# Attention and two MoE layers on one core: the last routing in another order with VectorE's subtractions, and the small tokens' block with its copy and its transposes moved

## The chip, the cores and the metric

The kernel runs on 1 core of a Trainium2 chip. The metric is the device time in microseconds (us) of one execution. Engines are called as in the profile: PE is TensorE, DVE is VectorE, ACT is ScalarE, POOL is GpSimd, SP is SyncE, which issues most DMAs. PSUM is the memory that PE writes; its banks are tiles such as `psT`, `psH`, `psO`, `psf`, `psR` here, and SBUF is the memory that the engines and the DMAs share.

## The reference

Attention over 4 x 8 heads of 576 positions with 64 columns each (half of the heads with a local mask, half with a strided one) gives 2304 tokens of 512 columns. Two mixture-of-experts layers follow, each with 8 experts of which a token takes one:

```python
def _moe_ref(x, w_skip, w_gate, w1, w2):            # layer 1
    do_compute = x @ w_skip > 0
    xc = x[do_compute]
    logits = xc @ w_gate
    e_idx = np.argmax(logits, axis=1)
    gate_w = softmax(logits)[arange, e_idx]
    for e in range(8):
        m = e_idx == e
        y[m] = gate_w[m, None] * (np.maximum(xc[m] @ w1[e], 0.0) @ w2[e])
    out = x.copy(); out[do_compute] = xc + y
def _moe2_ref(x, modality_id, w_gate, modality_bias, w1, w2):   # layer 2
    logits = x @ w_gate + modality_bias[modality_id]
    ...  # the same choice of one expert for every token, no residual
    out[m] = gate_w[m, None] * (np.maximum(x[m] @ w1[e], 0.0) @ w2[e])
```

w1 is 512 x 1024 and w2 is 1024 x 512 for each expert.

## The kernel before, in words

**Products.** A float32 number is split into two numbers of the type fp32r, a high and a low part: `x = xh + xl`, `w = wh + wl`. Each product is three matmuls: `wh` by `xh`, `wl` by `xh`, `wh` by `xl`. An expert's two weight matrices come as 8 pieces of 128 x 1024 numbers (512 KB). SP loads a piece into one of six buffers `raw`; `hi(c)` (L301) makes `wh` from it with a copy on ACT; `lo(c)` (L305) makes `wl` with the subtraction `raw - wh`, on DVE or on POOL, and then calls `ahead(1)`, which issues the load of a further piece into a buffer that has come free. `pieces(i)` gives the pairs of `hi` and `lo` of the weights number `i`.

**Stages.** Attention writes the tokens to DRAM (`xbuf`). A token that layer 1 skips goes on to layer 2 at once, so the routing also forms lists for layer 2. `drain` runs when attention's last tile is through; it covers about the stretch from 128 to 167 us. In it three things are interleaved by the turns of a loop. First, `route(1)`, the last routing: it is a generator, and each `next` runs it up to the next `yield`. It finds the greatest logit of each token as a one-hot matrix `r_oh` (L555 to L558), then counts on PE which place the token takes in its expert's list (`rk`, L565 to L571; `r_sel`, L574), then the gates (`r_gs`, `ent`), the number of tokens of each expert (`cnt`, L593) and the plan of the blocks (`plan1`), then the places `r_val`, `r_vi`, `r_pc`, then one-hot matrices of them (`ra`, L626, `r_b`, `rb`, L658) and by matmuls with these the lists of token numbers (`ls`, L643 and L664; `list`, L666). Between them, `later(n)` issues up to `n` small DVE instructions of the planning that were put off (all at L160). Second, `fill`, which works through two full tiles of the favourite expert of layer 2 (`psf`, `hfh`, `hfl`; matmuls L1455 and L1467). Third, 7 of the 8 pieces of the second weight slot, which layer 1 needs; `wstep()` runs one `hi` or one `lo`.

The loop of `drain` gives in each turn one step of the routing, two `wstep`s and as many groups of `fill` as `RUNS` says. Each engine runs its instructions in the order in which they are issued here. After `drain` the first block of layer 1 gathers the tokens `xgA` by the list, transposes them (`psT`, L1268), splits them (`xh` on ACT, `xl` on DVE, L1264) and multiplies (`psH`, `psO`, L1279).

**Few tokens.** A block of layer 1 has a tile of 128 tokens and, where an expert's list goes just beyond it, up to 32 "few" tokens. These go through the weights in float32, unsplit, beside the tile of the block (`few1`). `FEW1` says ahead of which matmul of the tile (0 to 47) each step of theirs stands. `timed` sorts all steps of a block by that number; steps with one number keep their order, and steps put off from the block before (`self.defer`) stand first among equals. Among these are the ranks of the few tokens of the block before (`carry`, L1621, which reads the bank `psT` of the few tokens, called T3 in the program) and its list (`list`, L1630, which reads the bank `psR`). Steps of the few tokens that matter here: `first` (L1125) copies their columns from `psR` to `x`; `l1` (L1130) multiplies by the first weights into the bank T3; `relu` (L1135) reads this bank on ACT, and then PE transposes `x` into the same bank (L1136); `trh` transposes the result of the relu (L1268). The loop body of a block runs for the kinds of blocks in `USUAL`; on these inputs three blocks have few tokens.

Of the kernel before, what the change touches and what calls it, by code (L numbers as in the profile page):

```python
# [65 lines left out]
HI1 = (0, 0, 7, 15, 21, 26, 35, 39)  # L66
LO1 = (1, 1, 10, 15, 25, 28, 37, 42)
TL1 = (6, 11, 22, 22, 24, 28, 32, 34, 45)
FEW1 = (0, 4, 4, 7, 9, 19, 21, 22, 24, 27, 31, 34, 34, 37, 47)
MISC1 = (8, 22, 27, 41, 43)  # L70
RAW6 = 11
SOON = (0, 0, 1, 1, 1, 2, 1, 1, 0)
# [1 line left out]

USUAL = ("one", "one", "two", "one", "few", "few", "few", "one")
KINDS = [{"one": (62, 0), "two": (63, 2), "few": (62, MARK)}[n] for n in USUAL]
RUNS = (1, 3, 2, 3, 1, 2, 6, 4, 4, 3)
SLOTS = ("A0", "B0", "A1", "B1", "C0", "C1")
FIRST, REST = (("A1", "B1"), ("A0", "B0")), ("C0", "C1")
OUT = float(2 ** 23)  # L80
# [1 line left out]
SBT = NTILE // 2  # L82
# [84 lines left out]
class Net:  # L167
# [255 lines left out]
    def drain(self, fill):  # L423


        tc = self.tc
        self.inx.close()
        pool = self.ctx.enter_context(tc.tile_pool(name="slot1", bufs=1, side="right", reuse_waits="tile"))
        self.wsl[1] = [self.whalf(1, i, pool) for i in range(2)]
        self.raw += [pool.tile([P, FF], F32, name=f"raw{i}", tag=f"raw{i}") for i in range(3, 6)]  # L430
        self.ahead(3)
        self.rp = self.flx.enter_context(tc.tile_pool(name="rt", bufs=1, reuse_waits="tile"))
        self.wside = [op for p in self.pieces(1, pool=range(8))[:7] for op in p]
        runs = list(RUNS)
        while self.side or self.rside:
            self.step(1 - self.ofree)
            self.wstep()
            self.wstep()
            self.run(fill, runs.pop(0) if runs else 3)
        self.run(fill, 99)  # L440
        while self.wside:
            self.wstep()
        self.flx.close()
        self.apx.close()

# [81 lines left out]
    def route(self, sb, lt):  # L527

        nc, ps, ap = self.nc, self.ps, self.ap
# [6 lines left out]
        def t(nm, w, dt=F32):  # L536
            return self.sm("r_" + nm, w, dt, pool=ap)
# [34 lines left out]
                         self.offb.unsqueeze(1).to_broadcast([P, SBT, W]), start=False, stop=True)  # L572
        sel = t("sel", [SBT, W])
        nc.vector.tensor_tensor(sel.rearrange("p j n -> p (j n)"), rk, ohf, op=ALU.mult)  # L574

        gs, ent = t("gs", [SBT, 2]), self.ent[:, j0:j0 + SBT]
        nc.vector.tensor_reduce(gs.rearrange("p j g -> p (j g)"), fl(ex), axis=AX.X, op=ALU.add)
# [10 lines left out]
        else:  # L588
            with nc.allow_low_precision("small integers"):
                nc.vector.tensor_reduce(self.carry, oh.rearrange("p j n -> p n j"), axis=AX.X, op=ALU.add)  # L590
        yield 1
        o4 = self.obank(f"cnt{sb}")
        nc.tensor.matmul(o4[:, :2 * E], self.onb, self.carry, start=True, stop=True)  # L593
        if sb:
            cnt = self.sm("cnt", 2 * E, pool=self.rp)
            nc.vector.tensor_copy(cnt, o4[:, :2 * E])
            self.plan1(cnt)
            yield 1
        else:
            m = self.sm("c_n", E + 1)  # L600
            nc.vector.scalar_tensor_tensor(m[:, :E], o4[:, E:2 * E], 0.0, self.foh, ALU.add, ALU.mult, accum_out=m[:, E:])
            nc.vector.tensor_scalar(self.full, self.cst("thr")[:, 1:1 + FULL], m[:, E:], None, ALU.is_le)
            nc.vector.tensor_reduce(self.nfull, self.full, axis=AX.X, op=ALU.add)
        val, vi, pc = t("val", SBT), t("vi", [3, SBT], I32), t("pc", [2, SBT])
        later = self.bg.issue
        nc.vector.tensor_reduce(val, sel, axis=AX.X, op=ALU.add)
        later(2)
        nc.vector.tensor_copy(vi[:, 0], val)
        later(2)
        nc.vector.tensor_scalar(vi[:, 1], vi[:, 0], P - 1, None, ALU.bitwise_and)  # L610
        later(2)
        nc.vector.tensor_scalar(vi[:, 2], vi[:, 0], 7, None, ALU.logical_shift_right)
        later(2)
        nc.vector.tensor_copy(pc, vi[:, 1:])
        later(2)
        yield 1
# [13 lines left out]
        if sb:  # L630

            b0, b1 = t("b0", [SBT, NTILE]), t("b1", [SBT, NTILE], F32R)
            nc.vector.tensor_tensor(b0, bc(col, NTILE), iota[:, :NTILE].unsqueeze(1).to_broadcast([P, SBT, NTILE]),
                                    op=ALU.is_equal)
            later(2)
            nc.vector.tensor_tensor(b1, b0, bc(tid, NTILE), op=ALU.mult)
            later(2)
            for g in range(ng):
                mk_a(g)
            yield 1  # L640
            o3 = self.obank("ls0")
            for j in range(SBT):
                nc.tensor.matmul(o3[:, :NTILE], aa[j // n][:, j % n], b1[:, j], start=j == 0, stop=j == SBT - 1)  # L643
            f = t("f", [2, NTILE])
            nc.vector.tensor_tensor(f[:, 0], self.list1[:, :NTILE], o3[:, :NTILE], op=ALU.add)
            later(2)
            nc.vector.tensor_scalar(f[:, 1], f[:, 0], 0.0, self.cst("dummy"), ALU.is_equal, ALU.mult)
            later(2)
            nc.vector.scalar_tensor_tensor(self.li[0], f[:, 0], -1.0, f[:, 1], ALU.add, ALU.add)
            later(2)  # L650
            self.gather("A0", self.li[0][:, 0:1])
        for g in range(ng):
            bb = []
            if not sb:
                mk_a(g)
            for j in range(g * n, g * n + n):
                b = ap.tile([P, NC2], F32R, name=f"rb{sb}{j}", tag="rb", bufs=n)
                nc.vector.tensor_scalar(b, iota, col[:, j:j + 1], tid[:, j:j + 1], ALU.is_equal, ALU.mult)  # L658
                later(2)
                bb.append(b)  # L660
            yield 1
            o3 = self.obank(f"ls{sb}{g}")
            for i, b in enumerate(bb):
                nc.tensor.matmul(o3[:, :NC2], aa[g][:, i], b, start=i == 0, stop=i == n - 1)  # L664
            if sb or g:
# [446 lines left out]
    def few1(self, k, free):  # L1112

        nc, b, Q, i = self.nc, self.bk["T3"], 2 * P, k % 2
        xg, ix = self.xs[f"C{i}"]["g"], self.fwi[:, 2 * i:2 * i + 1]

        t = self.xs[f"B{1 - i}"]["g"]
        hs, y, x = t[:, :Q], t[:, Q:Q + P], t[:, Q + P:Q + 2 * P]
# [245 lines left out]
    def tile_few(self, k, slot, idx, conv, start, end):  # L1364
# [519 lines left out]
```

## Time and profile before

| | |
|---|---|
| time, median of 3 runs | 566.18 us (562.84 to 567.45) |
| the profiled execution | 565.65 us |
| its span, first to last instruction | 563.8 us |
| mean granted clock of PE, as a share of full speed | 0.966 |
| busy: PE, DVE, ACT, POOL | 503.2, 326.2, 244.2, 112.0 us |

The difference of 1.85 us between the profiled execution and its span lies outside the instructions. The chain that ended last is made up of 55% PE, 16% DVE, 12% DMA, 8% issue and 7% ACT. PE is busy for most of the span, but the shares are averages over stages. In `drain` and at the ends of blocks other engines set the pace, and there PE waits.

### The profile page before, as it was taken

How to read it: one execution, taken by the hardware profiler on the slowest of the kernel's cores; microseconds unless marked ns; L12 is line 12 of the kernel's file. 1: busy time of each engine (PE TensorE's matmuls, PEld its weight loads, DVE VectorE, ACT ScalarE, POOL GpSimd, SP SyncE). 2: the span in 40 equal slices, each digit the busy share in tenths (PEclk: the TensorE clock that was granted, in tenths of full speed). 3: DMA queues.
4: the chain of work that ended last, by engine and by line, in shares of the span. 5: the costliest groups of instructions: out<-in, count | busy, mean ns of one | idle time of the engine just before them, and what ended most of it. 6: DMA issues, size and time to landing. Idle time of an engine off the chain costs nothing.

```text
span 563.8 us, 11022 instructions
## 1 busy us (share of the span) xinstructions
PE 503.2 (89%) x3959; PEld 398.7 (71%) x3959; DVE 326.2 (58%) x909; ACT 244.2 (43%) x539; POOL 112.0 (20%) x129
## 2 busy tenths in 40 slices
PE   5998998986687989999898987989999999999992
PEld 2677666775575669666565666979987788899981
DVE  1567689747879689696967795656522122223121
ACT  0888696653227556366456562135211121111120
POOL 4200000106515222122202032041211202020210
PEclk9999899998889899999999998989999999999997
DMA  8996885326517788387656575038231741120110
GB/s 205 341 337 205 255 284 181 90 73 237 155 38 257 270 289 270 130 292 227 208 187 223 169 234 199 20 121 287 85 80 44 258 179 39 40 76 20 58 41 20
DMA packets 32807, 94.76 MB, mean 168 GB/s; under 512 B 6192, under 2 KB 11282, under 8 KB 32720
## 3 DMA queue, kind: packets, MB, share of 16 engines
q1 hardware_dynamic: 26464, 75.23, 40.6%
q0 software_dynamic: 5824, 18.01, 9.7%
q8 instruction: 39, 0.64, 0.5%
q10 hardware_dynamic: 432, 0.49, 0.4%
q14 instruction: 48, 0.39, 0.2%
HBM read 81.72 MB, written 12.62 MB: 167 GB/s over the span
## 4 chain that ended last, share of the span: by engine, by line
PE 55%; DVE 16%; DMA 12%; issue 8%; ACT 7%; POOL 1%; DVEq 0%; ACTq 0%; POOLq 0%
PE psH L1455 11%; PE psT L1467 7%; PE psO L1467 7%; DMA xgB<-xbuf,li 6%; PE psH L1279 4%; PE psT L1455 4%; DVE wl L305 3%; PE psT L1268 3%; PE o L1778 2%; PE pt L1760 2%; DMA xbuf<-x1p,pidx 2%; ACT p L1749 2%; PE psf L1455 2%; DMA neg<-in_neg 1%; ACT wh L301 1%
## 5 line engine op out<-in xcount | busy, mean ns | idle before, releaser
L305 DVE TENSOR_TENSOR wl<-raw,wh 128x1024 fp32r<-128x1024 f32 (+1 forms) x89 | 98.9, 1123 | 17.4 <-ACT wh L301 17.2
L301 ACT CAST wh<-raw 128x1024 fp32r<-128x1024 f32 (+1 forms) x96 | 96.0, 1021 | 7.1 <-issue 4.3
L1461 ACT ACTIVATE hh<-psH 128x256 fp32r<-128x256 f32 x45 | 17.3, 384 | 94.0 <-PE psH L1455 94.0
L1462 DVE SCALAR_TENSOR_TENSOR hl<-psH,hh 128x256 fp32r<-128x256 f32 x45 | 18.9, 424 | 63.3 <-ACT hh L1461 63.3
L1749 ACT ACTIVATE p<-s,mx 128x96 f32<-128x96 f32 (+2 forms) x152 | 41.2, 373 | 0.9 <-DVE r L1785 0.9
L1455 PE MATMUL psH<-xl,wh 128*128 128x256 f32 x192 | 32.4, 289 | 2.0 <-DVE xl L1264 2.0
L1455 PE MATMUL psH<-xh,wl 128*128 128x256 f32 x192 | 33.5, 291 | 0.2 <-issue 0.2
L1455 PEld LDWEIGHTS psH<-xh,wh 128*128 128x128 f32 x192 | 29.2, 191 | 4.4 <-ACT xh L1263 1.0
L1763 ACT COPY pts<-pt 96x512 f32<-96x512 f32 (+4 forms) x48 | 22.9, 495 | 21.0 <-PE pt L1760 20.5
L1455 PE MATMUL psH<-xh,wh 128*128 128x256 f32 x192 | 31.1, 284 | 0.8 <-ACT xh L1263 0.8
L1455 PEld LDWEIGHTS psH<-xl,wh 128*128 128x128 f32 x192 | 27.1, 194 | 3.0 <-DVE xl L1264 2.4
L1455 PEld LDWEIGHTS psH<-xh,wl 128*128 128x128 f32 x192 | 27.6, 196 | 1.5 <-issue 1.5
L1424 POOL DMA_INDIRECT out_dram<-x1p,li x8 | 8.0, 1004 | 96.1 <-DVE x1p L1423 94.2
L1467 PE MATMUL psO<-wh,hh 128*128 128x512 f32 x60 | 25.1, 419 | 0.0
L1279 PE MATMUL psO<-wh,hl 128*128 128x512 f32 x72 | 24.2, 429 | 0.8 <-DVE hl L1264 0.8
L1602 POOL DMA_INDIRECT xbuf<-x1p,pidx x8 | 8.9, 1114 | 79.3 <-DVE xgB L1609 42.9
L1279 PE MATMUL psO<-wl,hh 128*128 128x512 f32 x72 | 24.6, 425 | 0.0
L1264 DVE TENSOR_TENSOR xl<-psT,xh 128x512 fp32r<-128x512 f32 x29 | 19.9, 688 | 8.1 <-ACT xh L1263 8.1
L1279 PE MATMUL psH<-wl,xh 128*128 128x512 f32 x72 | 24.5, 421 | 0.0
L1760 PE MATMUL pt<-cst,p 128*96 128x128 f32 (+2 forms) x152 | 23.5, 276 | 0.9 <-ACT xT L1813 0.9
L1467 PE MATMUL psT<-wh,hh 128*128 128x512 f32 x60 | 23.9, 398 | 0.0
L1467 PE MATMUL psT<-wh,hl 128*128 128x512 f32 x60 | 23.7, 395 | 0.0
(451 smaller groups left out, 1164.5 us busy)
## 6 DMA issues: line engine op xcount, KB each, us to landing
raw<-in_w SPq DMA_DIRECT2D x104, 512.0 KB
qk<-in_lqk SPq DMA_DIRECT2D x8, 592.0 KB
qk<-in_sqk SPq DMA_DIRECT2D x8, 576.0 KB
v<-in_lv SPq DMA_DIRECT2D x8, 438.8 KB
v<-in_sv SPq DMA_DIRECT2D x8, 325.0 KB
xbuf<-xl SPq DMA_DIRECT2D x4, 576.0 KB
xbuf<-xs SPq DMA_DIRECT2D x12, 108.0 KB
xbuf<-xs SPq DMA_DIRECT2D x8, 126.0 KB
```

Of the source, the lines that this page charges most:

```text
L301: nc.scalar.copy(placed(wh[:, c % 4, q], c), turned(self.rawtile(8 * i + c)[:, q], c))
L305: (nc.gpsimd if c in pool else nc.vector).tensor_tensor(placed(wl[:, c % 4, q], c), turned(self.rawtile(8 * i + c)[:, q], c), placed(wh[:, ...
L1264: nc.vector.tensor_tensor(l, src, h.bitcast(F32), op=ALU.subtract)
L1268: self.nc.tensor.transpose(bank[:, k * P:(k + 1) * P], src[:, k * P:(k + 1) * P], self.ident)
L1279: return [lambda i=i, a=a, b=b: self.nc.tensor.matmul(out, a, b, start=first and i == 0, stop=last and i == n - 1) for i, (a, b) in enumer ...
L1455: return [lambda i=i, k=k, w=w, x=x: nc.tensor.matmul(hb[f % nb], w[:, k, c], x[:, k], start=i == 0 and k == 0, stop=i == 2 and k == 3) fo ...
L1461: nc.scalar.activation(h, hb[f % nb], AF.Relu)
L1462: nc.vector.scalar_tensor_tensor(l, hb[f % nb], 0.0, h.bitcast(F32), ALU.max, ALU.subtract)
L1467: return [lambda i=i, j=j: nc.tensor.matmul(ob[t], hp[i][:, c], m[j], start=f == 0 and i + j == 0, stop=f == FF // P - 1 and i == 1) for i ...
L1749: nc.scalar.activation(self.p[:rows, h, c], self.s[:rows, h, c], AF.Exp, scale=0.125, bias=self.mx[:rows, h, n:n + 1])
L1760: nc.tensor.transpose(pt[:w, (n - n0) * rows:(n - n0 + 1) * rows], self.p[:rows, h, n * w:(n + 1) * w], net.ident[:rows, :rows])
L1763: nc.scalar.copy(pts[:w, :m * rows], pt[:w, :m * rows])
```

## The change

The change has two parts. In `drain` the seven subtractions of the second weight slot run on DVE and no longer on POOL, and three tables say how many groups of `fill`, copies and subtractions each turn has. The last routing (`sb` = 1) works out the tokens' places right after `r_sel`; the gates come after them, and the count matmul and the plan come after the one-hot matrices. `later(4)` takes the place of `later(2)` behind each `rb` and each `list`.

In the few tokens' block, `first` has the number -1, so that it stands ahead of the steps that were put off with number 0; `trh` has 11 where it had 9; and in `relu` PE's transposing of `x` is issued ahead of ACT's relu.

```diff
-FEW1 = (0, 4, 4, 7, 9, 19, 21, 22, 24, 27, 31, 34, 34, 37, 47)
+FEW1 = (-1, 4, 4, 7, 11, 19, 21, 22, 24, 27, 31, 34, 34, 37, 47)
...
-RUNS = (1, 3, 2, 3, 1, 2, 6, 4, 4, 3)
+
+RUNS = (1, 3, 2, 3, 4, 5, 5, 5)
+HIS = (0, 1, 1, 1, 1, 1, 1, 1)
+LOS = (0, 0, 1, 0, 1, 1, 2, 2)
...
-        self.wside = [op for p in self.pieces(1, pool=range(8))[:7] for op in p]
-        runs = list(RUNS)
+        his, los = [list(ops) for ops in zip(*self.pieces(1)[:7])]
+        runs = [*zip(RUNS, HIS, LOS)]
         while self.side or self.rside:
+            n, nh, nl = runs.pop(0) if runs else (3, 7, 7)
             self.step(1 - self.ofree)
-            self.wstep()
-            self.wstep()
-            self.run(fill, runs.pop(0) if runs else 3)
+            for ops, m in ((his, nh), (los, nl)):
+                for op in ops[:m]:
+                    op()
+                del ops[:m]
+            self.run(fill, n)
...
         nc.vector.tensor_tensor(sel.rearrange("p j n -> p (j n)"), rk, ohf, op=ALU.mult)
+        val, vi, pc = t("val", SBT), t("vi", [3, SBT], I32), t("pc", [2, SBT])
+        later = self.bg.issue
+
+        def places():
+            nc.vector.tensor_reduce(val, sel, axis=AX.X, op=ALU.add)
+            nc.vector.tensor_copy(vi[:, 0], val)
+            nc.vector.tensor_scalar(vi[:, 1], vi[:, 0], P - 1, None, ALU.bitwise_and)
+            nc.vector.tensor_scalar(vi[:, 2], vi[:, 0], 7, None, ALU.logical_shift_right)
+            nc.vector.tensor_copy(pc, vi[:, 1:])
+        if sb:
+
+            places()
...
             for g in range(ng):
                 mk_a(g)
+            yield 1
+            o4 = self.obank(f"cnt{sb}")
+            nc.tensor.matmul(o4[:, :2 * E], self.onb, self.carry, start=True, stop=True)
+            cnt = self.sm("cnt", 2 * E, pool=self.rp)
+            nc.vector.tensor_copy(cnt, o4[:, :2 * E])
+            self.plan1(cnt)
             yield 1
...
                 nc.vector.tensor_scalar(b, iota, col[:, j:j + 1], tid[:, j:j + 1], ALU.is_equal, ALU.mult)
-                later(2)
+                later(4)
...
         def relu():
+            nc.tensor.transpose(b[:, P + Q:], x, self.ident)
             nc.scalar.activation(self.halves(hs), self.turn(h), AF.Relu)
-            nc.tensor.transpose(b[:, P + Q:], x, self.ident)
             nc.scalar.copy(y, b[:, P + Q:])
```

Line numbers after the change are 3 to 8 higher. On DVE in `drain`, around the one-hot `r_oh` of the last routing, before:

```order
L557 TENSOR_TENSOR r_eq<-r_eq,r_mx 128x144
L558 TENSOR_TENSOR r_oh<-r_eq,r_act 128x144
L1462 SCALAR_TENSOR_TENSOR hfl<-psf_1828,hfh 128x256
L574 TENSOR_TENSOR r_sel<-rk_2010,r_oh 128x144
L577 TENSOR_REDUCE r_gs<-r_ex 128x18
L578 TENSOR_SCALAR r_gs<-r_gs 128x18
```

The same place on DVE now:

```order
L563 TENSOR_TENSOR r_eq<-r_eq,r_mx 128x144
L564 TENSOR_TENSOR r_oh<-r_eq,r_act 128x144
L308 TENSOR_TENSOR wl_1938<-raw_70,wh_1937 128x1024
L1470 SCALAR_TENSOR_TENSOR hfl<-psf_1828,hfh 128x256
L580 TENSOR_TENSOR r_sel<-rk_2005,r_oh 128x144
L585 TENSOR_REDUCE r_val<-r_sel 128x9
L586 CAST r_vi<-r_val 128x9
```

The first subtraction (`wl`) has come in behind `r_oh`, ahead of the split `hfl` and of `r_sel`, and the places `r_val`, `r_vi` follow `r_sel` where the gates `r_gs` followed.

On DVE at the end of `drain`, from the last `rb` to the last `list` (the names at L160 are the put-off planning), before:

```order
L658 TENSOR_SCALAR rb_2269<-csta,r_pc 128x288
L160 TENSOR_REDUCE f_v<-f_junk 128x1
L160 TENSOR_TENSOR f_junk<-c_foh,cnt 128x8
L666 TENSOR_TENSOR list_118<-list_118,ls_2284 128x288
L160 TENSOR_REDUCE f_m<-f_junk 128x1
```

The same place on DVE now:

```order
L666 TENSOR_SCALAR rb_2255<-csta,r_pc 128x288
L163 TENSOR_REDUCE f_v<-f_junk 128x1
L163 TENSOR_TENSOR f_junk<-c_foh,cnt 128x8
L163 TENSOR_REDUCE f_m<-f_junk 128x1
L163 SCALAR_TENSOR_TENSOR f_m<-c_nfull,f_m 128x1
L308 TENSOR_TENSOR wl_1940<-raw_1943,wh_1939 128x1024
L308 TENSOR_TENSOR wl_1940<-raw_70,wh_1939 128x1024
L674 TENSOR_TENSOR list_118<-list_118,ls_2286 128x288
```

The last two of the seven subtractions stand between the last `rb` and the last `list`; behind that come the rest of the planning and then `xl` of the first block, as before.

On PE in a block with few tokens, from the last few-token matmul of the first weights to the transposes of `trh` (the `psT_2313` written from `xgB` is the bank T3), before:

```order
L1130 MATMUL psT_2313<-raw_68,xgB_2331 32x256 x4
L1279 MATMUL psH_2316<-wl_65,xh_2337 128x512 x2
L1268 MATMUL psT_2310<-cst,x1p 128x128 x4
L1279 MATMUL psH_2316<-wl_65,xh_2337 128x512
L1136 MATMUL psT_2313<-cst,xgB_2331 128x128
L1279 MATMUL psH_2316<-wl_65,xh_2337 128x512
L1279 MATMUL psH_2316<-wh_64,xl_2342 128x512
L1268 MATMUL psT_2313<-cst,xgB_2331 128x128 x2
```

The same place on PE now:

```order
L1138 MATMUL psT_2313<-raw_68,xgB_2331 32x256 x4
L1287 MATMUL psH_2316<-wl_65,xh_2337 128x512 x2
L1276 MATMUL psT_2310<-cst,x1p 128x128 x4
L1287 MATMUL psH_2316<-wl_65,xh_2337 128x512
L1143 MATMUL psT_2313<-cst,xgB_2331 128x128
L1287 MATMUL psH_2316<-wl_65,xh_2337 128x512
L1287 MATMUL psH_2316<-wh_64,xl_2342 128x512 x3
L1276 MATMUL psT_2313<-cst,xgB_2331 128x128 x2
```

The transposing of `x` stands at the same place among PE's instructions, but it no longer waits for the relu, which now waits for it; the two transposes of `trh` stand behind four of the tile's matmuls where they stood behind two. On POOL, the seven rows of L305 ahead of the gather of `xgA` (L1254) are gone. On ACT the copy L1125 stands where it stood.

## Rows read from the trace of the kernel before

**Rows 1.** Part 1 of the page: busy time, share of the span, instructions.

```profile
PE 503.2 (89%) x3959; PEld 398.7 (71%) x3959; DVE 326.2 (58%) x909; ACT 244.2 (43%) x539; POOL 112.0 (20%) x129
```

**Rows 2.** Timeline of PE, 128 to 190 us: start, us, instructions, [idle before <-releaser].

```profile
137.51 0.30 PE L565 MATMUL rk<-r_oh,ltb 128*128 128x144 bf16 x1 [5.40 <-DVE r_oh L558]
...
153.85 2.26 PE L643 MATMUL ls<-r_b,ra 128*128 128x18 f32 x9 [4.54 <-DVE ra L626]
...
183.10 0.66 PE L1268 MATMUL psT<-cst,xgA 128*128 128x128 f32 x4 [3.03 <-DMA xgA<-xbuf,li]
```

**Rows 3.** Timeline of POOL, 125 to 185 us.

```profile
127.52 9.77 POOL L305 TENSOR_TENSOR wl<-raw,wh 128x1024 fp32r<-128x1024 f32 x4 [16.71 <-ACT wh L301]
144.16 7.09 POOL L305 TENSOR_TENSOR wl<-raw,wh 128x1024 fp32r<-128x1024 f32 x3 [6.87 <-ACT wh L301]
...
175.40 1.72 POOL L1254 DMA_INDIRECT xgA<-xbuf,li  x1 [4.03 <-DVE li L821]
```

**Rows 4.** DVE by source line: xcount, ns min/median/max, first and last start, forms.

```profile
L555 DVE SCALAR_TENSOR_TENSOR r_eq<-r_L,cst x2: 309/1373/2437, 83.4 to 130.2; 128x144 f32<-128x144 f32 x2
...
L557 DVE TENSOR_TENSOR r_eq<-r_eq,r_mx x2: 309/1178/2048, 84.1 to 133.0; 128x144 f32<-128x144 f32 x2
...
L558 DVE TENSOR_TENSOR r_oh<-r_eq,r_act x2: 307/1345/2383, 84.4 to 135.1; 128x144 bf16<-128x144 f32 x2
...
L612 DVE TENSOR_SCALAR r_vi<-r_vi x2: 165/1278/2391, 90.4 to 148.9; 128x9 int32<-128x9 int32 x2
...
L160 DVE TENSOR_TENSOR more<-more,one x2: 153/1262/2370, 144.2 to 151.2; 128x8 f32<-128x8 f32 x2
...
L160 DVE TENSOR_SCALAR one<-f x1: 2324/2324/2324, 146.6 to 146.6; 128x8 f32<-128x8 f32 x1
```

**Rows 5.** Windows: start:end, us, busy PE, PEld, DVE, ACT, POOL, PEclk, DMA share, GB/s.

```profile
129.11:169.23 40.12, 28.48 (x143) 24.10 (x142) 32.83 (x107) 10.39 (x16) 17.88 (x10) 0.83 0.42 139
...
180.70:184.10 3.40, 1.00 (x7) 0.92 (x8) 2.43 (x5) 1.73 (x3) 0.60 (x3) 1.00 0.96 363
184.10:187.50 3.40, 3.40 (x11) 2.31 (x9) 2.52 (x3) 0.87 (x2) 0.00 (x0) 0.50 1.02 402
```

**Rows 6.** Groups by line and form: xcount, busy us, mean ns of one, idle before.

```profile
L305 DVE TENSOR_TENSOR wl<-raw,wh 128x1024 fp32r<-128x1024 f32 x73 | 87.9, 1219 | 14.6 <-ACT wh L301 14.5
...
L305 POOL TENSOR_TENSOR wl<-raw,wh 128x1024 fp32r<-128x1024 f32 x7 | 16.9, 2445 | 23.6 <-ACT wh L301 23.6
```

**Rows 7.** Waits of DVE, 129.11 to 169.23 us: us in total, times, longest us.

```profile
DVE hfl L1462 <- ACT hfh L1461: 4.9, 3, 2.4
DVE list L666 <- PE ls L664: 1.3, 3, 0.7
DVE r_sel L574 <- PE rk L571: 0.8, 1, 0.8
```

**Rows 8.** Waits by source line, L1135 and L1125: who waited for them (us, times).

```profile
  PE psT L1136: 2.4, 3
...
  PE psT L1130: 4.5, 3
```

**Rows 9.** Timeline of PE, 272 to 284 us, a block with few tokens.

```profile
277.23 1.93 PE L1130 MATMUL psT<-raw,xgB 128*32 128x256 f32 x32 [1.71 <-ACT xgB L1125]
...
281.28 0.33 PE L1136 MATMUL psT<-cst,xgB 128*128 128x128 f32 x1 [0.79 <-ACT xgB L1135]
...
282.22 0.72 PE L1279 MATMUL psH<-wh,xl 128*128 128x512 f32 x2
```

**Rows 10.** Timeline of DVE and ACT, 270 to 285 us, the same block.

```profile
275.83 0.29 DVE L1630 TENSOR_TENSOR list<-list,psR 128x144 f32<-128x144 f32 x1
...
276.98 0.14 DVE L1621 TENSOR_TENSOR carry<-carry,psT 128x8 f32<-128x8 f32 x1
...
276.16 0.27 ACT L1125 COPY xgB<-psR 128x128 f32<-128x128 f32 x1 [2.46 <-DVE list L1630]
280.84 0.39 ACT L1135 ACTIVATE xgB<-psT 128x256 f32<-128x256 f32 x1
```

More of the change, by code (lines that the diff above doesn't have):

```diff
@@ L432, in drain @@
         self.rp = self.flx.enter_context(tc.tile_pool(name="rt", bufs=1, reuse_waits="tile"))
-        self.wside = [op for p in self.pieces(1, pool=range(8))[:7] for op in p]
-        runs = list(RUNS)
+        his, los = [list(ops) for ops in zip(*self.pieces(1)[:7])]
+        runs = [*zip(RUNS, HIS, LOS)]
         while self.side or self.rside:
+            n, nh, nl = runs.pop(0) if runs else (3, 7, 7)
             self.step(1 - self.ofree)
-            self.wstep()
-            self.wstep()
-            self.run(fill, runs.pop(0) if runs else 3)
+            for ops, m in ((his, nh), (los, nl)):
[3 more added lines that the diff above has]
+            self.run(fill, n)
         self.run(fill, 99)
-        while self.wside:
-            self.wstep()
+        for op in his + los:
+            op()
         self.flx.close()
@@ L590, in route @@
                 nc.vector.tensor_reduce(self.carry, oh.rearrange("p j n -> p n j"), axis=AX.X, op=ALU.add)
[L591 to L597, printed above, removed]
+        if not sb:
             yield 1
-        else:
+            o4 = self.obank(f"cnt{sb}")
+            nc.tensor.matmul(o4[:, :2 * E], self.onb, self.carry, start=True, stop=True)
             m = self.sm("c_n", E + 1)
@@ L603, in route @@
             nc.vector.tensor_reduce(self.nfull, self.full, axis=AX.X, op=ALU.add)
-        val, vi, pc = t("val", SBT), t("vi", [3, SBT], I32), t("pc", [2, SBT])
-        later = self.bg.issue
-        nc.vector.tensor_reduce(val, sel, axis=AX.X, op=ALU.add)
-        later(2)
[L608 to L616, printed above, removed]
+            places()
+            yield 1
         n, ng = 3, SBT // 3
@@ L640, in route @@
             yield 1
+            o4 = self.obank(f"cnt{sb}")
+            nc.tensor.matmul(o4[:, :2 * E], self.onb, self.carry, start=True, stop=True)
+            cnt = self.sm("cnt", 2 * E, pool=self.rp)
+            nc.vector.tensor_copy(cnt, o4[:, :2 * E])
+            self.plan1(cnt)
+            yield 1
             o3 = self.obank("ls0")
@@ L658, in route @@
                 nc.vector.tensor_scalar(b, iota, col[:, j:j + 1], tid[:, j:j + 1], ALU.is_equal, ALU.mult)
-                later(2)
+                later(4)
                 bb.append(b)
@@ L666, in route @@
                 nc.vector.tensor_tensor(self.list1[:, :NC2], self.list1[:, :NC2], o3[:, :NC2], op=ALU.add)
-                later(2)
+                later(4)
             else:
                 nc.vector.tensor_copy(self.list1[:, :NC2], o3[:, :NC2])
-                later(2)
+                later(4)
         if not sb:
```

## The prediction, made before the change was run

> **What bounds the kernel now.** I read the busy shares first: PE is busy 503.2 of the span [rows 1], so time can only be won where PE stands still or where it is slowed. The timeline of PE shows such places in `drain`: it stands 5.40 us ahead of `rk`, for DVE's `r_oh`, and 4.54 us ahead of the first `ls`, for DVE's `ra` [rows 2]. So in `drain` the bound is DVE's chain of routing instructions. In the window from the first of them to the start of the first block's `xl`, 40.12 us, DVE is busy 32.83 us and PE 28.48 at a mean clock of 0.83 [rows 5].
>
> The next view tells why DVE is so busy. The same source lines run twice in the kernel, for each routing once. `r_eq`, `r_oh` and their like take 0.31 us in the one and 2.05 to 2.44 in the other; small instructions of 0.15 to 0.17 us take 2.32 to 2.39 there [rows 4]. These six long ones start between 130.2 and 149 us, all inside the two runs of POOL's subtractions, 127.52 to 137.3 and 144.16 to 151.25 [rows 3], and none is longer than one such subtraction, 2.445 us [rows 6]. I take it that POOL's subtraction holds DVE's instruction back until it is through.
>
> Behind `drain` the lead must not be lost again. PE's next long wait is 3.03 us for the second gather of `xgA` [rows 2], which POOL issues after 4.03 us of waiting for DVE's `li` [rows 3]. So what comes early there is what DVE's chain makes early; a PE that arrives earlier than that only waits longer.
>
> **Subtractions from POOL to DVE.** Released are the excesses of the six instructions, maximum less minimum of each row, and for the sixth, which ran once, less 0.165 of its like: 2.13 + 1.74 + 2.08 + 2.23 + 2.22 + 2.16 = 12.55 us [rows 4]. Added are seven subtractions of 1.219 us [rows 6], 8.53 us. DVE's work in the window is then 32.83 - 12.55 + 8.53 = 28.81 us. Of its idle 7.29 us, 7.0 are waits in three groups: 4.9 for ACT's `hfh`, 1.3 for PE's `ls`, 0.8 for `rk` [rows 7]; 0.29 are small gaps and stay. If no wait stays, the window takes 29.1 us and 11.0 are saved; if all stay, 36.1 and 4.0 are saved. In the new order a subtraction stands between `r_oh` and `r_sel`, which covers the 0.8, and subtractions stand ahead of three of the `hfl`, 3.66 us against the 4.9, which leaves 1.24. I let the 1.3 at `ls` stay whole. Then 2.5 stay, the window takes 31.6 us, and **8.5 us** are saved. PE's work in the window, 28.5 us with two stretches at half clock in it, is shorter than this and loses its two long waits; it stays beside DVE's.
>
> The other moves of this part cost little by themselves. The places go ahead of the gates, five short instructions ahead of seven, so `ra` and the first `ls` come earlier on DVE's chain; the sum above has all of this inside, as it counts work and not order. The count and the plan come later; what waits for them are the put-off instructions, which have no waiter before the end of `drain`. SP's loads of further weight pieces follow each subtraction, and the last two subtractions stand behind the last `rb`, some 2 us before `xl`. They put 2.4 us ahead of the last `list` and `xl`, and their two loads come late beside the start of the first block. The 2.4 is in the sum of DVE's work; the loads are in a rival below. POOL loses 16.9 us of work [rows 6] and nobody waits for it in `drain`, so its gathers come no later.
>
> **Relu and transposes.** PE's transpose (L1136) waits for ACT's relu three times, 2.4 us together [rows 8], once 0.79 [rows 9]. After the change it waits for nothing but PE's own work, which was through at 281.28 - 0.79 = 280.49. The relu then waits for it. It started at 280.84 [rows 10] because ACT came to it then, later than such a transpose needs, so the relu still ends at about 281.23. What is late next is `trh`, which reads the relu's result. It stands behind four matmuls now; two take 0.72 us [rows 9], so four take 1 us at least with the transpose, and end past 281.4: no wait. I count the whole 2.4 less 0.05 for handing over, **2.35 us**. The bounds are 0, if the wait only moves to `trh`, and 2.4.
>
> **The copy ahead of put-off work.** The waits by source line give 4.5 us in three waits of PE for the copy L1125 [rows 8], 1.71 of it in the block shown [rows 9]. That suggests a gain, but the rows say otherwise. The copy started at 276.16, right behind DVE's `list` of 275.83 to 276.12, on which it waited 2.46 us, and it ended at 276.43; PE's matmul began only at 277.23, behind `carry` (276.98 to 277.12), which reads the bank that the matmul writes [rows 10]. Neither `list` nor `carry` is moved, and on ACT the copy stands where it stood. I count **0**; the other end is -4.5, nearer to nothing in these rows.
>
> The waits view and a rule differ here, in sentences that the sum can do without. The Trainium skill, PSUM — Partial Sum Buffer, section "PSUM bank collisions raise a hardware error", says that accesses of two engines to one bank must be kept apart by a semaphore per bank, reads against reads too. By the waits view alone the edit would be worth up to 4.5 us; by that rule the copy has to wait for the reader of `psR` and the matmul for the reader of T3, wherever the copy is written. The trace agrees with the rule by the 0.11 us between `carry`'s end and the matmul's start.
>
> **The sum**, against the profiled execution of 565.65 us (0.5 below the median of 566.18, which I take as the same): 565.65 - 8.5 - 2.35 + 0 = **554.8 us**.
>
> **Rivals.** (B) The start of layer 1 gives part back. From 180.70 to 184.10 PE was busy 1.00 us of 3.40, and the 3.40 us behind it ran at half clock with PE busy throughout [rows 5]. That is 1.7 us lost. At the end of `drain` PE now has two subtractions of DVE to sit through and may be as sparse, and the last loads of weights come later. One or two such stretches cost 1.7 to 3.4 us: 556.5 to 558.2. Against it speaks that `drain` had two stretches at half clock, of which one may go. The Trainium skill, TensorE: Matmul & The Clock Gate, section "HAM oscillation — how this bites in real kernels", describes the same as a rule: a PE that waits for data is put back to 1.2 GHz (of 2.4) and starts its next work slow; the trace agrees by the clock of 0.50 behind the sparse stretch.
>
> (C) DVE's waits all stay, because subtractions wait for ACT's `wh` (they did for 14.6 us in 73 cases, 0.2 each [rows 6]) and the `hfl` for PE as before. Then 4.0 are saved: 565.65 - 4.0 - 2.35 = 559.3.
>
> (D) More goes than I count: no wait stays on DVE, 565.65 - 11.0 - 2.35 = 552.3, and with the 4.5 of the copy 547.8. For it: the waits of `hfl` come from a PE that was itself held up or at half clock.
>
> (E) The other side: POOL is not what stretches DVE's instructions; they wait for something else that stays. Then DVE's unbroken chain gets 8.53 us more, 565.65 + 8.53 - 2.35 = 571.8, or 566.9 if the 4.9 of `hfl` take some of it up. It decides from the point where less than 8.5 of the 12.55 us are released. Against it: six of six long instructions lie beside POOL's work.
>
> (F) The edit doesn't do what it says: the copy comes no earlier. This is in the forecast.
>
> **How the numbers follow.** My forecast has 55%, with a range of its own of 552.5 to 556.5; B 18%, C 9%, D 8%, E 3%, and 7% for what I don't see. The range holds the forecast, B and C, 82%: 550 to 560 us, its low end between D's two values. A measurement of this kernel tells about 1%, 5.7 us, from no change. Below 560.5 lie the forecast, B, D and nearly all of C: 88% faster. Within 1% are the rest of C, half of E and part of the unseen, 8%; slower 4%.
>
> **What would show it.** In the profile after: `r_eq`, `r_oh`, `r_vi` at 0.31 and 0.17 us in both routings; seven more DVE subtractions of about 1.2; the window from DVE's first routing instruction to `xl` 31 to 32 us long; no wait of 4 us or more of PE in `drain`; the second gather of `xgA` 8 to 9 us earlier; no wait of PE for L1135's relu; PE's wait at the few-token matmul unchanged at 4 to 5 us in three. It would be wrong if small DVE instructions are still stretched, if `wl` on DVE waits for `wh` by several us, or if the blocks of layer 1 are longer by half-clock stretches than before.

## The result

The changed kernel takes 549.98 us (median of 4 runs, 548.6 to 551.21) beside 565.72 us before: ratio 0.9726, 95% interval 0.9676 to 0.9776. Timed again (e9), it gave 0.9729 (0.9677 to 0.978). That is some 15 us or 2.7% faster, where 554.8 us was forecast. It lies at the very edge of the range of 550 to 560 us: the median is 0.02 us below it, and the ratio applied to the 565.65 us of the forecast gives 550.2.

### The profile page after: what moved, and what is told of

It reads as the page before. It is cut to its first block, busy times and chain, and to the rows that moved or that the text cites. A ratio compares the mean times of both kernels' runs of the same rounds, so it can differ in the third digit from the quotient of the medians.

```text
span 549.1 us, 11013 instructions
## 1 busy us (share of the span) xinstructions
PE 496.1 (90%) x3958; PEld 393.9 (72%) x3959; DVE 322.0 (59%) x916; ACT 244.2 (44%) x539; POOL 94.2 (17%) x122
## 4 chain that ended last, share of the span: by engine, by line
PE 42%; DMA 10%; DVE 8%; issue 7%; ACT 2%; POOL 1%; DVEq 0%; POOLq 0%; ACTq 0%
PE psH L1463 11%; DMA xgB<-xbuf,li 7%; PE psT L1475 7%; PE psO L1475 7%; PE psH L1287 5%; PE psT L1463 4%; PE psT L1276 3%; DVE wl L308 3%; DMA xbuf<-x1p,pidx 2%; PE psT L1155 1%; PE psT L1138 1%; PE psO L1287 1%; ACT hh L1271 1%; PE psR L1092 1%; PE psR L1078 1%
## 5 line engine op out<-in xcount | busy, mean ns | idle before, releaser
L308 DVE TENSOR_TENSOR wl<-raw,wh 128x1024 fp32r<-128x1024 f32 (+1 forms) x96 | 107.3, 1130 | 13.7 <-ACT wh L304 13.0
L1463 PE MATMUL psH<-xh,wh 128*128 128x256 f32 x192 | 30.5, 281 | 0.8 <-ACT xh L1271 0.8
L1262 POOL DMA_INDIRECT xgA<-xbuf,li x13 | 14.3, 1101 | 69.4 <-DVE more L163 30.2
L1287 PE MATMUL psH<-wh,xl 128*128 128x512 f32 x72 | 24.3, 437 | 0.0
L1271 ACT CAST xh<-psT 128x512 fp32r<-128x512 f32 x29 | 16.9, 585 | 16.7 <-PE psT L1276 16.2
```

Source lines behind the costliest of these rows:

```text
L308: (nc.gpsimd if c in pool else nc.vector).tensor_tensor(placed(wl[:, c % 4, q], c), turned(self.rawtile(8 * i + c)[:, q], c), placed(wh[:, ...
L1271: nc.scalar.copy(h, src)
L1287: return [lambda i=i, a=a, b=b: self.nc.tensor.matmul(out, a, b, start=first and i == 0, stop=last and i == n - 1) for i, (a, b) in enumer ...
L1463: return [lambda i=i, k=k, w=w, x=x: nc.tensor.matmul(hb[f % nb], w[:, k, c], x[:, k], start=i == 0 and k == 0, stop=i == 2 and k == 3) fo ...
```

## The profile after

Part 1 of the page after, to compare with [rows 1]: POOL has lost 17.8 us of work, yet DVE, which took seven subtractions over, is busy 4.2 us less than before (322.0, from 326.2).

```profile
PE 496.1 (90%) x3958; PEld 393.9 (72%) x3959; DVE 322.0 (59%) x916; ACT 244.2 (44%) x539; POOL 94.2 (17%) x122
```

The same DVE lines as in [rows 4], after (count, ns min/median/max, first and last start, forms): the two routings now take the same time, 0.31 and 0.16 us, where the last one took 2.05 to 2.44.

```profile
L561 DVE SCALAR_TENSOR_TENSOR r_eq<-r_L,cst x2: 308/308/309, 82.3 to 129.0; 128x144 f32<-128x144 f32 x2
...
L563 DVE TENSOR_TENSOR r_eq<-r_eq,r_mx x2: 309/310/310, 83.0 to 129.7; 128x144 f32<-128x144 f32 x2
...
L588 DVE TENSOR_SCALAR r_vi<-r_vi x2: 162/164/165, 89.3 to 132.7; 128x9 int32<-128x9 int32 x2
```

The windows after, to [rows 5]: first the stretch from DVE's first routing instruction to the first block's `xl`, then two stretches of half clock. The columns are start:end, length, busy PE, PEld, DVE, ACT, POOL, granted clock, DMA share, GB/s.

```profile
127.99:158.36 30.37, 25.66 (x146) 20.85 (x145) 28.81 (x113) 13.43 (x19) 3.82 (x6) 0.94 0.49 162
154.90:161.70 6.80, 6.12 (x15) 4.62 (x15) 6.13 (x16) 5.15 (x6) 2.83 (x5) 0.51 0.63 211
171.90:175.30 3.40, 2.79 (x9) 2.30 (x10) 1.24 (x4) 0.59 (x1) 0.00 (x0) 0.52 1.03 409
```

The stretch lasts 30.37 us where it lasted 40.12. DVE works 28.81 us of it, the very number of the sum, and stands 1.56. The waits of DVE in it are down from 7.0 us [rows 7] to this:

```profile
DVE hfl L1470 <- ACT hfh L1469: 0.8, 1, 0.8
```

PE after, to [rows 2] (start, us, instructions, [idle before <-releaser]): `rk` and the first `ls` wait for nothing worth a bracket, where they waited 5.40 and 4.54 us. The wait that comes next is the forecast one, for the second gather of `xgA`, 0.7 us longer than before, so PE arrived earlier still than the gather.

```profile
130.84 0.24 PE L571 MATMUL rk<-r_oh,ltb 128*128 128x144 bf16 x1
...
137.72 1.06 PE L651 MATMUL ls<-r_b,ra 128*128 128x18 f32 x9
...
172.51 1.11 PE L1276 MATMUL psT<-cst,xgA 128*128 128x128 f32 x4 [3.71 <-DMA xgA<-xbuf,li]
```

From DVE's first routing instruction to this row it is 44.52 us now and was 53.99: 9.47 us are won up to here. PE in the same block with few tokens as in [rows 9]:

```profile
268.52 1.93 PE L1138 MATMUL psT<-raw,xgB 128*32 128x256 f32 x32 [1.71 <-ACT xgB L1133]
...
271.31 0.48 PE L1287 MATMUL psH<-wl,xh 128*128 128x512 f32 x1
271.62 0.27 PE L1143 MATMUL psT<-cst,xgB 128*128 128x128 f32 x1
...
272.73 0.44 PE L1276 MATMUL psT<-cst,xgB 128*128 128x128 f32 x2
```

The wait at the copy is what it was, 1.71 us; the transpose no longer waits for the relu, and neither does `trh`. DVE and ACT there, to [rows 10]: the copy still starts behind `list` and the matmul still behind `carry`.

```profile
267.12 0.30 DVE L1638 TENSOR_TENSOR list<-list,psR 128x144 f32<-128x144 f32 x1
...
268.27 0.14 DVE L1629 TENSOR_TENSOR carry<-carry,psT 128x8 f32<-128x8 f32 x1
```

```profile
267.45 0.27 ACT L1133 COPY xgB<-psR 128x128 f32<-128x128 f32 x1 [2.46 <-DVE list L1638]
```

## The experiments

Theory: POOL's subtractions, lying beside DVE's routing, held DVE's instructions back, and DVE's chain set the pace; the few tokens' edit is worth PE's wait for the relu and no more. Rivals: the new order of the routing and the tables did it, with POOL a bystander; or the copy ahead of put-off work counts. All ratios below are to the kernel before, timed beside the experiment, and each is good to some 0.4 to 0.6%, 2 to 3 us.

### Which part, and which edit of it

**e1_drain_only**: the changed kernel, few tokens as before.

```diff
-FEW1 = (-1, 4, 4, 7, 11, 19, 21, 22, 24, 27, 31, 34, 34, 37, 47)
+FEW1 = (0, 4, 4, 7, 9, 19, 21, 22, 24, 27, 31, 34, 34, 37, 47)
...
-            nc.tensor.transpose(b[:, P + Q:], x, self.ident)
             nc.scalar.activation(self.halves(hs), self.turn(h), AF.Relu)
+            nc.tensor.transpose(b[:, P + Q:], x, self.ident)
```

> The changed kernel with the few tokens' edit undone, so the part in drain alone. Theory (POOL's subtractions held DVE's instructions back, and the relu wait is worth 1.05 us in each of three blocks): 11 to 13 us faster than the kernel before, about 3 us slower than the changed kernel; DVE's stretch from the first routing instruction to xl is 30 to 31 us. Rival (the drain gave only the 8.5 us of the prediction, the rest came from the few tokens' copy): 8 to 9 us faster.

**e2_few_only**: the kernel before, with the reverse of these lines and nothing else.

> The kernel before with the few tokens' edit alone (copy at -1, trh at 11, transpose ahead of relu). Theory: 3.1 us faster (1.05 in each of three blocks), PE's wait for the copy as long as before, 4 to 5 us in three. Rival (the copy counts as well): 5 to 7.5 us faster and the wait for the copy shorter.

**e3_new_order_pool** and **e4_old_order_dve**: order and engine taken apart. Of the lines, the first pair is e3 against the changed kernel, the second e4 against the kernel before.

```diff
-        his, los = [list(ops) for ops in zip(*self.pieces(1)[:7])]
+        his, los = [list(ops) for ops in zip(*self.pieces(1, pool=range(8))[:7])]
...
-        self.wside = [op for p in self.pieces(1, pool=range(8))[:7] for op in p]
+        self.wside = [op for p in self.pieces(1)[:7] for op in p]
```

> The changed kernel with the seven subtractions given back to POOL, all in the new order. Theory (it is POOL's work beside DVE's that costs): DVE instructions of 2 to 2.4 us again, of which six or seven cost 12 us, and the lead over the kernel before shrinks to 3 to 6 us, of which 3 are the few tokens'. Rival (the order and the tables do it, POOL is only a bystander): as fast as the changed kernel or faster by up to 8 us, as DVE is then rid of 8.5 us of work.

> The kernel before with the seven subtractions on DVE and nothing else changed. Theory: no stretched DVE instruction, DVE's stretch in drain shorter by 4 to 8 us, 4 to 8 us faster than the kernel before. Rival (order and tables do it): no faster, or slower by up to 8 us.

| kernel | order in drain | subtractions | few-token edit | ratio (95% interval) | DVE, first routing instruction to `xl` |
|---|---|---|---|---|---|
| before | old | POOL | no | 1 | 40.12 us |
| e2 | old | POOL | yes | 0.9953 (0.9906 to 1.0) | 39.67 us |
| e3 | new | POOL | yes | 0.9965 (0.9924 to 1.0006) | 40.78 us |
| e4 | old | DVE | no | 0.9835 (0.9778 to 0.9891) | 30.86 us |
| e1 | new | DVE | no | 0.9829 (0.9777 to 0.9882) | 30.66 us |
| after | new | DVE | yes | 0.9726 (0.9676 to 0.9776) | 30.37 us |

The last column has two values, 40 and 30.5 us, and the engine alone decides between them. In time the new order gains nothing that shows, with POOL (e3 against e2) or with DVE (e1 against e4). In e4 one of the seven subtractions stands ahead of the stretch, 1.2 us of work, and DVE's waits in it are 2.7 us where e1 has 0.8; so the order may be worth 1.4 us of the stretch (30.86 + 1.22 - 30.66, an estimate). The places put ahead of the gates, the count put back, the tables and `later(4)` are worth no more than that; the drain's gain comes from the argument `pool`. In e4, as in the profile after, no instruction of the last routing takes more than 0.6 us. The rival is out.

The times hit the expectations less well than the stretches do. e1 is 9.7 us faster (6.7 to 12.6), between its theory of 11 to 13 and its rival of 8 to 9, and can't tell them apart; that rival falls with e6 below. e4, 9.3 us, gained more than the 4 to 8 expected, and e3's lead of 2.0 us is short of the 3 to 6.

In e3 the long instructions have come to lie elsewhere, since POOL's work has moved. Its window, DVE and POOL:

```profile
130.22:171.00 40.78, 26.27 (x142) 21.89 (x141) 36.23 (x106) 11.16 (x17) 18.76 (x9) 0.83 0.42 138
```

```profile
131.25 2.44 DVE L561 SCALAR_TENSOR_TENSOR r_eq<-r_L,cst 128x144 f32<-128x144 f32 x1
...
134.06 2.05 DVE L563 TENSOR_TENSOR r_eq<-r_eq,r_mx 128x144 f32<-128x144 f32 x1
...
146.23 9.99 DVE L163 SCALAR_TENSOR_TENSOR pl_key<-cnt,cst 128x8 f32<-128x8 f32 x1
```

```profile
130.94 5.00 POOL L308 TENSOR_TENSOR wl<-raw,wh 128x1024 fp32r<-128x1024 f32 x2 [23.06 <-ACT wh L304]
...
146.82 9.37 POOL L308 TENSOR_TENSOR wl<-raw,wh 128x1024 fp32r<-128x1024 f32 x4
```

POOL's first two subtractions meet two routing instructions there, of 2.44 and 2.05 us; `r_oh`, behind POOL's work, is short again. The third row is a hold four times as long: `pl_key`, an instruction of 0.16 us in the profile after, ends at 156.22, when all four of POOL's subtractions (146.82 to 156.19) are through. So one hold need not end with one subtraction of POOL, as all six did before. Why DVE came in between POOL's subtractions there and not in this one execution, no run shows.

### POOL's work added back as a bystander

**e10_pool_bystander**: the changed kernel, and behind each copy of `drain` POOL subtracts the copy from itself into a scratch tile that nobody reads.

```diff
+        junk = self.rp.tile([P, DM], F32, name="junk", tag="junk")
+
+        def beside(c, op):
+            op()
+            wh = self.wsl[1][c // 4][0][:, c % 4].bitcast(F32)
+            for i in range(0, FF, DM):
+                self.nc.gpsimd.tensor_tensor(junk, wh[:, i:i + DM], wh[:, i:i + DM], op=ALU.subtract)
+        his = [lambda c=c, op=op: beside(c, op) for c, op in enumerate(his)]
```

> The changed kernel with useless work on POOL: behind each of the seven copies of drain POOL subtracts the copy from itself into a scratch tile, in two instructions of 512 columns, as much as the seven subtractions that it did before. No result depends on it and DVE's order is the same. Theory (POOL's reading beside DVE holds DVE's instructions back): DVE instructions with two inputs of 1 us and more beside it, DVE's stretch in drain 5 to 12 us longer, the kernel 5 to 12 us slower than the changed one. Rival (POOL's work was harmless, the gain came from elsewhere): within 1 us of the changed one.

Measured 0.9954 (0.9916 to 0.9991), 563.23 us beside 550.79 of the changed kernel (e9): 12.4 us slower, just beyond the 5 to 12 expected. DVE's stretch grew from 30.37 to 42.95 us: 10.0 us of it are DVE's instructions taking longer (38.82 us busy, from 28.81), 2.6 are more waits. Nothing else was added, so this prices the mechanism by itself: the holds, and the waits that they bring about. The timelines of POOL and of DVE show it instruction by instruction; POOL's row of 133.63 is one of the six in the first row, shown by itself:

```profile
130.13 7.86 POOL L443 TENSOR_TENSOR junk<-wh 128x512 f32<-128x512 f32 x6 [18.98 <-ACT wh L304]
...
133.63 2.12 POOL L443 TENSOR_TENSOR junk<-wh 128x512 f32<-128x512 f32 x1
...
138.21 2.15 POOL L443 TENSOR_TENSOR junk<-wh 128x512 f32<-128x512 f32 x2 [0.23 <-ACT wh L304]
```

```profile
130.44 1.03 DVE L569 SCALAR_TENSOR_TENSOR r_eq<-r_L,cst 128x144 f32<-128x144 f32 x1
131.51 0.30 DVE L570 TENSOR_REDUCE r_mx<-r_eq 128x18 f32<-128x144 f32 x1
131.85 0.75 DVE L571 TENSOR_TENSOR r_eq<-r_eq,r_mx 128x144 f32<-128x144 f32 x1
132.63 1.08 DVE L572 TENSOR_TENSOR r_oh<-r_eq,r_act 128x144 bf16<-128x144 f32 x1
133.63 1.21 DVE L308 TENSOR_TENSOR wl<-raw,wh 128x1024 fp32r<-128x1024 f32 x1
...
135.10 0.29 DVE L588 TENSOR_TENSOR r_sel<-rk,r_oh 128x144 f32<-128x144 f32 x1
...
138.25 1.03 DVE L604 TENSOR_SCALAR r_gs<-r_gs 128x18 f32<-128x18 f32 x1
139.32 0.27 DVE L605 RECIPROCAL r_gs<-r_gs 128x18 f32<-128x18 f32 x1
...
149.26 1.68 DVE L163 SCALAR_TENSOR_TENSOR pl_key<-cnt,cst 128x8 f32<-128x8 f32 x1
```

POOL's instruction is less than half as long here, 1.04 us in the median, and so are the holds: 0.75 to 1.08 us where they were 2.05 to 2.44, and 1.68 for `pl_key`. The reduction takes 0.30 us in the midst of POOL's work, as long as ever, and `r_sel`, which has one input in PSUM, 0.29. The hold works the other way too: DVE's subtraction of 133.63 takes its usual 1.21 us, and POOL's instruction of the same start takes 2.12 in place of 1.04.

### The few tokens' edit

**e5_relu_only** (the kernel before with the two lines of `relu` swapped), **e6_copy_only** (the first entry of `FEW1` from 0 to -1) and **e7_few_no_copy** (lines swapped and the fifth entry from 9 to 11).

For e6, and for e7 beside the swap:

```diff
-FEW1 = (0, 4, 4, 7, 9, 19, 21, 22, 24, 27, 31, 34, 34, 37, 47)
+FEW1 = (-1, 4, 4, 7, 9, 19, 21, 22, 24, 27, 31, 34, 34, 37, 47)
```

```diff
-FEW1 = (0, 4, 4, 7, 9, 19, 21, 22, 24, 27, 31, 34, 34, 37, 47)
+FEW1 = (0, 4, 4, 7, 11, 19, 21, 22, 24, 27, 31, 34, 34, 37, 47)
```

> The kernel before with only PE's transpose put ahead of ACT's relu; trh stays at 9. Theory (the relu wait is worth 1.05 us a block, trh must stand later so that the wait doesn't move there): PE's wait for the relu at the transpose is gone but a wait of 0.2 to 0.6 us turns up at trh, so 0.4 to 0.8 us a block, 1.2 to 2.4 us in all. Rival (the swap is all there is): 3.1 us and no wait at trh.

> The kernel before with only the few tokens' copy put ahead of the put-off work (0 to -1). Theory (nothing moves): the time of the kernel before, within 0.5%, and PE's wait for the copy 4 to 5 us in three as before. Rival (the copy is what PE waits for): up to 4.5 us faster and the wait gone.

> The kernel before with trh at 11 and the transpose ahead of the relu, the copy left at 0. Theory: as the few tokens' edit whole, 1.05 us in each of three blocks, 2 to 3.1 us faster than before. Rival (the copy counts): 2 us or more slower than with it.

Measured: e5 0.9999 (0.996 to 1.0038), e6 0.9999 (0.9948 to 1.005), e7 0.9945 (0.9904 to 0.9987). The copy is worth nothing that shows, and the edit without it is worth as much as with it (e2, 0.9953). The waits for L1125 in e6 say the same, to [rows 8]; PE waits for the copy as before:

```profile
  PE psT L1130: 4.4, 3
```

The swap alone doesn't show in the time, and its trace tells where most of its gain went. PE in the same block of e5:

```profile
282.05 0.27 PE L1135 MATMUL psT<-cst,xgB 128*128 128x128 f32 x1
...
283.15 0.44 PE L1268 MATMUL psT<-cst,xgB 128*128 128x128 f32 x2 [0.37 <-ACT xgB L1137]
```

The transpose waits no more, but `trh`, two matmuls behind it, now waits, 0.35 to 0.37 us in each of the three blocks. The two numbers of the edit belong together: the swap takes the wait away, and 11 for 9 keeps it from turning up again. From the few tokens' matmuls with the first weights to those with the second, e5 wins 0.5 to 0.6 us a block, 1.6 in all, as expected (in the second block after taking off 1.6 us that these matmuls, 3.51 us in place of 1.93, took longer), and the timing, good to 0.4%, can't tell that from nothing.

### Two attempts to go on, and the change again

**e8_gather_ahead**: the changed kernel with the wait of 3.71 us for the second gather attacked, by putting DVE's copy of its list and the gather ahead of the block's own subtractions.

```diff
-MISC0 = (8, 19, 31, 39, 43, 47, 13, 37, 24)
+MISC0 = (0, 19, 31, 39, 43, 47, 13, 37, 24)
```

> The changed kernel with the first block's list and gathers for the next block (the first entry of MISC0) put ahead of the block's own subtractions, from matmul 8 to 0. In the changed kernel PE waits 3.71 us for that gather, whose list DVE copies behind three subtractions. Theory (DVE's chain still sets the pace there): the gather is issued about 2.3 us earlier, PE's wait falls to 1.4 us or less and the kernel is 1 to 2.3 us faster than the changed one. Rival (the gather is held up by its registers or by DMAs that fill the queues, or the weights come late instead): no faster, within 1 us.

Measured 0.9791 (0.9735 to 0.9846): no faster than the changed kernel. Counted from the first block's transposes, `psT` is 3.2 us earlier at this gather than in the profile after, and 11 us later 0.2 us of that are left (0.7 further on). PE in e8:

```profile
167.62 0.66 PE L1276 MATMUL psT<-cst,xgA 128*128 128x128 f32 x4 [0.51 <-DMA xgA<-xbuf,li]
170.39 0.66 PE L1276 MATMUL psT<-cst,xgB 128*128 128x128 f32 x4 [1.18 <-DMA xgB<-xbuf,li]
173.00 0.40 PE L1117 MATMUL psR<-cst,xgC 32*128 32x32 f32 x4 [1.03 <-DMA xgC<-xbuf,fwi]
174.18 1.17 PE L1287 MATMUL psH<-wh,xh 128*128 128x512 f32 x4 [0.34 <-issue]
178.77 0.39 PE L1287 MATMUL psH<-wh,xh 128*128 128x512 f32 x1 [1.12 <-issue]
```

The wait for the first gather fell from 3.71 to 0.51; in its place PE waits for the gathers behind it, 1.18 and 1.03 us, and 1.46 for nothing that the profile names. The rival held; which of its causes it was stays open.

**e11_few_later** and **e12_few_bit_later**: the changed kernel with the few tokens' matmuls later, so that matmuls of the tile stand in the 1.7 us for `carry`; first e11, then e12.

```diff
-FEW1 = (-1, 4, 4, 7, 11, 19, 21, 22, 24, 27, 31, 34, 34, 37, 47)
+FEW1 = (-1, 10, 10, 13, 17, 23, 24, 25, 27, 29, 32, 35, 35, 38, 47)
```

```diff
-FEW1 = (-1, 4, 4, 7, 11, 19, 21, 22, 24, 27, 31, 34, 34, 37, 47)
+FEW1 = (-1, 7, 7, 10, 14, 20, 22, 23, 25, 28, 31, 34, 34, 37, 47)
```

> The changed kernel with the few tokens' steps later in the block: the first weights' matmuls from 4 to 10 and what follows them from 7 to 13, 11 to 17 and so on. Theory (PE's 1.7 us at these matmuls are a wait for DVE's carry and the copy behind DVE's list, and six of the tile's matmuls, 1.4 us, can stand in it): PE's wait falls from 4.7 us in three to under 1 us, 3 to 4.5 us faster than the changed kernel. Rival (weight buffers are freed later, so the wait turns into one for loads or for the results further on): no faster.

> The same by half: matmuls 4 to 7, 7 to 10, 11 to 14, and the steps behind by 0 to 1. Theory: three matmuls of 0.23 us stand in each wait, 2 us faster than the changed kernel. Rival: no faster.

Measured 0.9722 (0.9684 to 0.976) and 0.9783 (0.9737 to 0.983): e11 is as fast as the changed kernel, e12 no faster, so both theories missed. PE in e11, the same block:

```profile
267.67 0.66 PE L1276 MATMUL psT<-cst,x1p 128*128 128x128 f32 x4 [1.07 <-DVE xgB L1627]
269.20 1.93 PE L1138 MATMUL psT<-raw,xgB 128*32 128x256 f32 x32
```

The few-token matmul waits no more, but now the transposes of `x1p`, which had been shadowed by that wait, wait 1.07 us for DVE. From block to block the trace of e11 wins 0.7 to 1.0 us on the profile after, not 1.7, and the timing can't tell the 2.5 us that this makes in three.

**e9_after_again**: the changed kernel unaltered.

> The changed kernel unaltered, timed again beside the others of this call. Theory (the two parts add up: 10.4 us from the drain and 2 to 3.1 from the few tokens): 12.4 to 13.5 us faster than the kernel before, so the 15.7 of the first timing is at the upper end of its interval. Rival (the parts help each other): 15 to 16 us.

Measured 0.9729 (0.9677 to 0.978), 550.79 us beside 565.48: 14.7 us, between theory and rival. The two parts by themselves multiply to 0.9829 x 0.9953 = 0.9783, some 12 us of the 15. Their intervals are 0.5% to either side, so whether the parts add up or help each other stays open.

## Why the prediction was right, and what it missed

**POOL holds DVE back: right, and shown.** The excess of 12.55 us was read from two runs of the same lines; e10 gave 12.4 us back by adding POOL's work alone, and e3 and e4 showed the engine to be the cause and the order not. That the two numbers are alike proves nothing: in e10 the holds make 10.0 us and DVE's waits the rest. Rival E is out. The reading that no hold is longer than one subtraction fits the kernel before only; e3 has one of 9.99 us.

**The drain's sum: the work right, the idle time too large.** The predicted 28.81 us of DVE's work is what the trace after has. The step that was off is "then 2.5 stay": of the 7.0 us of waits, 0.8 stayed. The 1.3 at `ls` that I let stand whole went too. DVE's waits for PE and ACT were mostly made by DVE itself: PE was late with `psf` and `ls` because it had waited 5.40 and 4.54 us for DVE and worked at half clock behind each wait. The windows of the kernel before (columns as in [rows 5], the clock third from the end):

```profile
137.50:143.00 5.50, 5.49 (x29) 5.01 (x30) 2.11 (x10) 0.39 (x1) 0.00 (x0) 0.50 0.42 93
153.80:160.00 6.20, 6.13 (x25) 5.77 (x26) 4.91 (x27) 0.00 (x0) 1.10 (x1) 0.50 0.17 47
```

e10 bears this out: there DVE holds PE up again, and DVE's wait for `hfh` is back, though its subtractions stand where they stand in the changed kernel. The waits of PE and of DVE in e10's stretch:

```profile
PE cnt L652 <- DVE ohsum L613: 4.6, 1, 4.6
DVE hfl L1478 <- ACT hfh L1477: 3.3, 2, 2.5
```

So 9.75 us were saved where 8.5 were forecast, nearer to rival D than to C.

**Behind the drain: right.** DVE's chain set the next gather, 9.47 us earlier against the same start, not PE.

**Rival B came and cost nothing there.** PE did run at half clock (0.51) from 154.9 to 161.7 us, behind an end of `drain` in which it was busy 2.06 of 3.40 us (151.5 to 154.9), as B said. By the trace this cost nothing, as it lay ahead of PE's wait of 3.71 us for the gather, which took it up. The stretch of half clock behind that wait, 171.9 to 175.3, has its like in the kernel before, 184.1 to 187.5 [rows 5]. e8, which shortened the wait, had new waits behind it and shows no more.

**Relu: mechanism right, size too small.** The term was 2.35 us for three blocks. From the few tokens' matmuls with the first weights to those with the second it is 7.63 us in the block shown (268.52 to 276.15), where it was 8.69 (277.23 to 285.92), so 1.06; the other two blocks give 1.04 and 1.03, 3.1 in all. PE's wait of 0.79 [rows 9] is counted from the end that the profile gives to the matmul before. After, the transpose starts at 271.62, 0.31 us after the start of a matmul to which the profile gives 0.48: without a wait it would have started earlier than where the 0.79 begin. e2 and e7, 2.7 and 3.1 us, agree within their intervals (0 to 5.3 and 0.7 to 5.4). That 11 for 9 was needed is shown by e5.

**The copy: right.** e6 has no effect, and PE's wait in three blocks, 4.5 us before, is 4.4 in e6 and 4.7 in the profile after. In the block shown, `carry` ends at 268.41 and PE starts at 268.52.

**What is left.** The terms as measured in the traces, 9.5 and 3.1 us, make 12.6 of the 14.7 to 15.7 us. That would be a ratio of 0.978, at the upper end of both intervals, so some 2 us more may come from the change, and what would give them stays open. In the profiled pair the rest comes from stretches in which both kernels do the same. The changed kernel is 1.1 us ahead where `drain` begins, loses 2.8 us between the second gather and the first block with few tokens (68.9 us, from 66.1), and wins 3.9 us behind the last of these blocks (240.6 us to the end, from 244.4). With 9.5 us up to the gather and 3.0 over the few tokens' blocks this is the whole 14.7 us between the spans. Over the profiles of all kernels here but e8, which moved that gather, the first of these stretches takes 65.3 to 70.8 us, and over all of them the second 240.6 to 245.1, with kernels of the old and the new drain near both ends. So the profiled pair can't show them to be an effect of the change.

One wait makes most of the 2.8 us: DVE's `x1p` stood 3.09 us at 198.88 in the profile after (2.98 in e9) and 0.60 at 207.95 before. The profile names no releaser; the landing times fit the scatter of the tile before (`xbuf<-x1p`), which landed 4.3 us after POOL's end in the one, 3.8 in the other, and 3.3 in e1, where `x1p` did not wait at all. No experiment here ties this wait to the change.

**Where the range was lucky.** Its low end was put between D's two values, 552.3 and 547.8, and the lower one counted 4.5 us for the copy, which is worth nothing. Without it every case that the prediction worked out ends at 552.3 us or above, and the 549.98 measured lie below them all. The mechanisms were right; the saving was taken 1.25 us too small in the drain and 0.8 too small at the relu, and the rest lies in the stretches above or stays open.

## What to carry to other kernels

When the same source line runs twice in a kernel, compare its two durations: a small DVE instruction that takes as long there as the POOL work beside it is not slow but held, and moving POOL's work to DVE can then take DVE's time down, here 8.5 us of added work for 12.5 us of released work. Of an engine's waits in a stretch, ask which it has brought on itself by making others late; those went with the cause here. When a wait is taken from one instruction, look at who reads the result next and give it the same distance.

## What the runs showed of the hardware

Which DVE instructions POOL holds was not all expected. Beside POOL's subtractions of e10, instructions with two inputs in SBUF were held (0.31 to 1.03 us) unless DVE came first (the subtraction of 133.63), and so was a `TENSOR_SCALAR` of 18 columns with one input (0.18 to 1.03); a `TENSOR_REDUCE` (0.30), a `RECIPROCAL` (0.27, seen once) and `r_sel`, with one of two inputs in PSUM (0.29), were not. The Trainium skill, SBUF — State Buffer, section "Who interferes with whom", says that DVE and GpSimd share one pair of ports under an exclusive lock, that whichever issues first keeps it for the whole instruction while the other waits, that a DVE instruction with two SBUF inputs contends with a GpSimd instruction that reads SBUF and one in a two-port mode with GpSimd at large, and that `tensor_reduce` on trn2 never does. The traces agree on the two inputs, on `TENSOR_REDUCE` and on the lock in both directions; in which mode an instruction ran they do not show. Most holds are as long as what was left of one POOL instruction, at most 2.44 us beside 2.445 [rows 4, 6] and 1.08 beside 1.04 to 1.19, but the 9.99 us of e3 span four of 2.33 to 2.45 us in a row. There the wait was longer than one whole instruction, and the measurement stands.
